# A conformer block on one core: moving batch 1's QKV into batch 0's attention, and spacing the w_pw2 tiles of the convolution

## The chip, the core and the metric

The kernel runs on one core of a Trainium2 chip. The metric is the device time of one execution in microseconds; the median of the runs is compared.

## What is computed

The reference is one conformer block on x of shape (2, 1000, 512) in bfloat16: a feed-forward half step, self-attention with four heads of 128, a convolution module with a depthwise convolution of 31 taps, a second feed-forward half step, and a final layer norm. Cut to what matters:

```python
B, T, D, K, H = (2, 1000, 512, 31, 4)
def reference(x, w_ff1a, w_ff1b, w_qkv, w_o, w_pw1, dw, w_pw2, w_ff2a, w_ff2b):
    x = x + 0.5 * (silu(layernorm(x) @ w_ff1a) @ w_ff1b)          # FF1
    qkv = layernorm(x) @ w_qkv                                    # attention
    q, k, v = ...                       # (B, H, T, 128) each
    p = softmax(einsum('bhqd,bhkd->bhqk', q, k) * 128 ** -0.5)
    att = einsum('bhqk,bhkd->bhqd', p, v)                         # back to (B, T, D)
    x = x + att @ w_o
    h = layernorm(x) @ w_pw1                                      # convolution module
    h = h[..., :D] * sigmoid(h[..., D:])
    c = sum(pad(h)[:, i:i + T, :] * dw[i] for i in range(K))
    x = x + silu(c) @ w_pw2
    x = x + 0.5 * (silu(layernorm(x) @ w_ff2a) @ w_ff2b)          # FF2
    return layernorm(x)
```

## The kernel before

The kernel is written for the five engines directly. A helper records every instruction into a list for its engine (so in the profile nearly everything has line 91 or 111, and groups are told apart by their tiles); each engine works through its list in order, and waits on semaphores of the others. T is padded to 1024, so there are 16 row tiles of 128, eight for each batch, and four column blocks of 512 tokens (nb 0 and 1 are batch 0, nb 2 and 3 batch 1). The stages run one after the other: FF1, attention of batch 0, attention of batch 1, pointwise and depthwise convolution, FF2. The residual stays in SBUF (`xres`); the normed and transposed input of each stage is `hT`.

PSUM has eight banks. QKV uses banks 0 to 3 in a ring; the scores of a unit (one head, 128 queries) take two of the banks 0 to 5; the product with V (AV) of four heads takes bank 6 or 7; out-projection and the w_pw2 tiles use "y" banks.

The attention of one batch, cut: first QKV, then 32 units of scores and AV, the AV seven units behind the scores, then the out-projection.

```python
for b in range(B):
    if b > 0:
        K.wait("act", t_av_last[b - 1])           # q, k, v buffers are reused
    for lb in range(2):                           # 16 jobs: q and k of four heads
        nb = 2 * b + lb
        for hh in range(H):
            for which in range(2):
                sl = next_ring4("pe")
                ...                               # 4 matmuls wqkv x hT, 512 columns
                ... K.emit("act", "activation", qT or kT [:, hh, ...], bank(sl), ACT.Copy ...)
    for j in range(TPB):                          # 8 jobs: v of eight row tiles
        ...                                       # 4 matmuls hT x wqkv
        t_v = K.emit("act", "activation", v_sb[:, j, :], bank(sl), ACT.Copy, sem="act")

    def do_S(u):                                  # unit u = 4 * (query tile) + head
        ss = u % 3
        K.acquire_banks("pe", [2 * ss, 2 * ss + 1])
        ...                                       # 2 matmuls of 512 columns
        t1 = K.emit("dve", "tensor_reduce", nbias..., Sv[:, 0:T], AX.X, ALU.min, sem="dve")
        te = K.emit("act", "activation", Pbuf[psl][:, 0:T], Sv[:, 0:T], ACT.Exp, ...)
        if u % 2 == 1:                            # transposes two units' probabilities
            tp = K.emit("sp", "dma_start_transpose", PTpair[pts], Ppair[pts], sem="dsp")

    def do_AV(u):
        abank = 6 + (bq % 2)                      # bq: the query tile
        K.wait("pe", t_ptdma[u])
        if hh == 0:
            K.acquire_banks("pe", [abank])
        ...                                       # 8 matmuls of 128 columns
        if hh == H - 1:                           # after four heads
            ...                                   # dve: reciprocal, four tensor_scalar into atok
            ...                                   # sp: dma_start_transpose of atok into attT

    for step in range(NU + L):                    # NU = 32 units, L = 7
        if step < NU:
            do_S(step)
        if step - L >= 0:
            do_AV(step - L)
        hook(("unit", b, step))                   # batch 0: norms of row tiles 12 to 15

    for j in range(TPB):                          # out-projection of eight row tiles
        ...                                       # 4 matmuls attT x wo
        ...                                       # dve: add into xres; then norm statistics
```

The FF2 weights are loaded into the tiles `w_a` and `w_b`, which FF1 used, as soon as FF1 is done:

```python
ff_phase([], lambda i: tile_done(i, 12), ff1_hook)
rel1 = slab_release()
K.waits("sp", rel1)
t_w["w_a"] = [K.emit("sp", "dma_start", w_a[...], wav2[...], sem="dsp") for hf in range(2)]
t_w["w_b"] = K.emit("sp", "dma_start", w_b[:], ..., sem="dsp")
attn_phase(rel1, lambda i: tile_done(i, 12), attn_hook)
rel2 = slab_release()
conv_phase(rel2, lambda i: tile_done(i, 8), conv_hook)
```

The depthwise convolution runs in four iterations of 512 tokens. Each loads shifted copies of the gated input by DMA (`load_g4`, one iteration ahead), runs eight groups of 16 tap matmuls on PE, then a silu (four sigmoids on ScalarE, four products on VectorE). The w_pw2 tiles of the iteration before, which read its silu, are put between the tap groups:

```python
for it, (b, tb) in enumerate(iters):
    banks = [0, 1, 2, 3] if it % 2 == 0 else [4, 5, 6, 7]
    ybanks = [4, 5] if it % 2 == 0 else [0, 1]
    if it + 1 < len(iters):
        load_g4(it + 1)                           # waits for the taps of it - 1
    pend = ...                                    # the four w_pw2 tiles of it - 1
    K.acquire_banks("pe", banks)
    K.waits("pe", t_g4[it])
    for m in range(NTG):                          # NTG = 8 tap groups
        ...                                       # 16 matmuls
        if pend and m % 2 == 1:
            pw2_tile(pend.pop(0), ybanks)         # 4 matmuls, then dve adds into xres, norm
    for i in range(4):
        ts = K.emit("act", "activation", sig[:, ss, :], bank(banks[i]), ACT.Sigmoid, sem="act")
        tm = K.emit("dve", "tensor_tensor", sT[:, i, ...], bank(banks[i]), sig[:, ss, :], ALU.mult, sem="dve")
```

Of the kernel before, what the change touches and what calls it, by code (L numbers as in the profile page):

```python
# [5 lines left out]
ACT = mybir.ActivationFunctionType  # L6
# [5 lines left out]
B = 2  # L12
T = 1000
D = 512
KCONV = 31
H = 4
DH = D // H
TP = 1024
DC = D // 128
F = 4 * D  # L20
# [3 lines left out]
TPB = TP // 128  # L24
# [6 lines left out]
SCALE = float(DH) ** -0.5  # L31
# [105 lines left out]
def bass_standalone__conformer_family_zipformer__speech_kernel(  # L137
# [13 lines left out]
    with ExitStack() as es:  # L151
# [42 lines left out]
        attT = big[0][:, 0:H * B * TP].rearrange("p (h t) -> p h t", h=H)  # L194
        qT = big[1][:, 0:H * TP].rearrange("p (h t) -> p h t", h=H)
        kT = big[1][:, H * TP:2 * H * TP].rearrange("p (h t) -> p h t", h=H)
        dw_sb = big[2][:, 0:D]
        NP = 8
        Pbuf = [big[2][:, s_ * TP:(s_ + 1) * TP] for s_ in range(NP)]
# [11 lines left out]
        def bank(b):  # L211
            return ps[:, b, :]
# [31 lines left out]
        t_w = {}  # L244
# [165 lines left out]
        def hT_ready(eng, nb):  # L410
            for lt in range(4):
                K.wait(eng, t_tr[nb * 4 + lt])
# [68 lines left out]
        def attn_phase(slab_waits, on_tile_done, hook):  # L481
# [12 lines left out]
            t_attT = {}  # L494
            t_av_last = {}

            for b in range(B):
                if b > 0:
                    K.wait("act", t_av_last[b - 1])
                t_qk = None  # L500
                for lb in range(2):
                    nb = 2 * b + lb
                    for hh in range(H):
                        for which in range(2):
                            sl = next_ring4("pe")
                            hT_ready("pe", nb)
                            col0 = which * D + hh * DH
                            t = None
                            for kc in range(DC):
                                t = K.emit("pe", "matmul", bank(sl), wqkv[:, kc, col0:col0 + DH],  # L510
                                           hT[:, kc, nb * 512:(nb + 1) * 512],
                                           start=(kc == 0), stop=(kc == DC - 1),
                                           sem=("pe" if kc == DC - 1 else None))
                            hT_readers[nb].append(t) if (hh == H - 1 and which == 1) else None
                            K.wait("act", t)
                            if which == 0:
                                t_qk = K.emit("act", "activation", qT[:, hh, lb * 512:(lb + 1) * 512], bank(sl),
                                              ACT.Copy, scale=-SCALE, sem="act")
                            else:
                                t_qk = K.emit("act", "activation", kT[:, hh, lb * 512:(lb + 1) * 512], bank(sl),  # L520
                                              ACT.Copy, sem="act")
                            K.set_bank_readers([sl], [t_qk])
                t_v = None
                for j in range(TPB):
                    i = b * TPB + j
                    nb = i // 4
                    sl = next_ring4("pe")
                    hT_ready("pe", nb)
                    t = None
                    for kc in range(DC):  # L530
                        t = K.emit("pe", "matmul", bank(sl), hT[:, kc, i * 128:(i + 1) * 128],
                                   wqkv[:, kc, 2 * D:3 * D],
                                   start=(kc == 0), stop=(kc == DC - 1),
                                   sem=("pe" if kc == DC - 1 else None))
                    hT_readers[nb].append(t) if j % 4 == 3 else None
                    K.wait("act", t)
                    t_v = K.emit("act", "activation", v_sb[:, j, :], bank(sl), ACT.Copy, sem="act")
                    K.set_bank_readers([sl], [t_v])

                hook(("qkv", b))  # L540
                units = [(qt, hh) for qt in range(TPB) for hh in range(H)]
# [4 lines left out]
                def do_S(u):  # L546
                    qt, hh = units[u]
                    ss = u % 3
                    K.acquire_banks("pe", [2 * ss, 2 * ss + 1])
                    K.wait("pe", t_qk)  # L550
                    Sv = sview(ss)
                    t = None
                    for kb in range(2):
                        t = K.emit("pe", "matmul", Sv[:, kb * 512:(kb + 1) * 512],
                                   qT[:, hh, qt * 128:(qt + 1) * 128],
                                   kT[:, hh, kb * 512:(kb + 1) * 512],
                                   start=True, stop=True, sem=("pe" if kb == 1 else None))
# [12 lines left out]
                    if u % 2 == 1:  # L570
                        K.wait("sp", t_exp[u - 1])
                        K.wait("sp", te)
                        pts = psl // 2
                        K.waits("sp", pt_readers[psl - 1] + pt_readers[psl])
                        tp = K.emit("sp", "dma_start_transpose", PTpair[pts], Ppair[pts], sem="dsp")
                        p_readers[psl - 1] = [tp]
                        p_readers[psl] = [tp]
                        t_ptdma[u - 1] = tp
                        t_ptdma[u] = tp

                def do_AV(u):
                    qt, hh = units[u]
                    bq = b * TPB + qt
                    abank = 6 + (bq % 2)
                    pts = u % NPT
                    K.wait("pe", t_ptdma[u])
                    K.wait("pe", t_v)
# [3 lines left out]
                    t = None  # L591
                    for kc in range(TPB):
                        t = K.emit("pe", "matmul", av[:, hh * DH:(hh + 1) * DH], PT[pts][:, kc, :],
                                   v_sb[:, kc, hh * DH:(hh + 1) * DH],
                                   start=(kc == 0), stop=(kc == TPB - 1),
                                   sem=("pe" if kc == TPB - 1 else None))
                    pt_readers[pts] = [t]
# [63 lines left out]
        def conv_phase(slab_waits, on_tile_done, hook):  # L661
# [97 lines left out]
            for it, (b, tb) in enumerate(iters):  # L759
# [25 lines left out]
                t_taps[it] = t  # L785
                K.wait("act", t)
# [34 lines left out]
        def slab_release():  # L821
            return [("pe", K.cnt["pe"])] + [t_x[i] for i in range(NTILE)]
# [17 lines left out]
        def ff1_hook(ev):  # L840
# [4 lines left out]
            elif ev == ("ffa_done", 1):  # L845
                for i in range(12, 16):
# [4 lines left out]

        ff_phase([], lambda i: tile_done(i, 12), ff1_hook)
        rel1 = slab_release()
        K.waits("sp", rel1)
        wav2 = w_ff2a.rearrange("(kc p) f -> p kc f", p=128)
        t_w["w_a"] = [K.emit("sp", "dma_start", w_a[:, :, hf * (F // 2):(hf + 1) * (F // 2)],
                             wav2[:, :, hf * (F // 2):(hf + 1) * (F // 2)], sem="dsp") for hf in range(2)]
        t_w["w_b"] = K.emit("sp", "dma_start", w_b[:], w_ff2b.rearrange("(fc p) d -> p fc d", p=128), sem="dsp")

        def attn_hook(ev):  # L860
            if ev[0] == "unit" and ev[1] == 0 and ev[2] in (2, 4, 6, 8):
# [2 lines left out]
        attn_phase(rel1, lambda i: tile_done(i, 12), attn_hook)  # L864
        assert [d[0] for d in deferred] == [12, 13, 14, 15]
        rel2 = slab_release()

        def conv_hook(ev):
            if ev[0] == "pw1" and ev[1] in (1, 2):
# [48 lines left out]
```

## Time and profile before

| | |
|---|---|
| median of 4 runs | 572.95 us (572.51 to 574.88) |
| profiled span | 570.7 us |
| PE busy | 443.1 us, 78% |
| VectorE busy | 331.2 us, 58% |
| ScalarE busy | 264.6 us, 46% |
| GpSimd busy | 81.0 us, 14% |
| mean granted PE clock | 0.953 |

The stages in the profiled execution, from its timeline: FF1 to 148, attention of batch 0 from 148 to 244, attention of batch 1 from 244 to 334, the pointwise part of the convolution from 334 to 371, the taps from 376 to 435, FF2 from 440 to the end at 570.7 us.

In the lines of a profile, PE is TensorE's matmuls and PEld its weight loads, DVE is VectorE, ACT ScalarE, POOL GpSimd, and SPq the queue of SyncE that issues DMAs. A timeline line has the start, the duration, the engine, the program's line, the operation, the output and input tiles with their shape and the number of instructions merged; in square brackets stands the idle time before it and what ended it. `big` is any of four large buffers that different stages use for different things (in attention: q, k, the probabilities and their transposes; in the convolution: the gated input, its shifted copies and the silu). A busy share is an average; where an engine is in order, its idle time before one instruction tells more than its share.

### The profile page before, as it was taken

The numbers are of one execution on the slowest core, as the hardware profiler recorded it, in microseconds if no ns is written. First come the engines' busy times: TensorE is split into PE (matmuls) and PEld (weight loads), VectorE is DVE, ScalarE is ACT, GpSimd is POOL, SyncE is SP. The second block draws the span as 40 slices with busy tenths as digits, with TensorE's granted clock in tenths as the row PEclk, the third lists the DMA queues.
The fourth block names the chain that finished last, engine by engine and source line by source line (L and its number), as shares of the span: only waits on it lengthen the run. The fifth ranks groups of instructions, "written<-read, shape, count | busy, mean of one in ns | idle before, by whom it ended". The sixth has DMA issues, their size and how long they took to land. (4 is left out here: it accounts for less than half of the span.)

```text
span 570.7 us, 7590 instructions
## 1 busy us (share of the span) xinstructions
PE 443.1 (78%) x2673; PEld 203.6 (36%) x2720; DVE 331.2 (58%) x741; ACT 264.6 (46%) x428; POOL 81.0 (14%) x231
## 2 busy tenths in 40 slices
PE   1596999999995565788665687867877649999995
PEld 1242444334442344333343432333222214444442
DVE  4276765797219886633988355206534667575743
ACT  3656553432379764167876144202322455353522
POOL 3201311101002000220000023404400210202021
PEclk9998999999999998799999699879888999999998
DMA  8801150102447999320999632969910120001011
GB/s 280 270 2 37 39 165 20 28 1 46 162 134 130 175 176 175 65 48 0 187 179 181 117 47 36 205 110 175 184 29 1 28 46 2 28 2 37 1 35 45
DMA packets 125034, 51.75 MB, mean 91 GB/s; under 512 B 107653, under 2 KB 120900, under 8 KB 124996
## 3 DMA queue, kind: packets, MB, share of 16 engines
q1 hardware_dynamic: 123460, 46.84, 38.6%
q0 software_dynamic: 1536, 4.43, 3.8%
q8 instruction: 21, 0.34, 0.2%
q14 instruction: 17, 0.14, 0.1%
HBM read 14.14 MB, written 2.05 MB: 28 GB/s over the span
## 5 line engine op out<-in xcount | busy, mean ns | idle before, releaser
L111 DVE TENSOR_TENSOR big<-ps,sig 128x512 bf16<-128x512 f32 (+1 forms) x160 | 106.8, 686 | 79.1 <-ACT sig L111 78.9
L111 ACT ACTIVATE sig<-ps 128x512 bf16<-128x512 f32 x160 | 91.2, 595 | 79.3 <-PE ps L111 70.2
L91 PE MATMUL ps<-hT,w_a 128*128 128x512 bf16 x373 | 104.6, 389 | 20.9 <-DVE big L111 19.2
L91 PE MATMUL ps<-w_b,big 128*128 128x512 bf16 x470 | 107.8, 379 | 0.5
L111 DVE TENSOR_REDUCE nbias<-ps 128x1 f32<-128x1000 f32 x64 | 73.3, 1191 | 46.6 <-PE ps L111 46.5
L111 ACT ACTIVATE hbf<-xres,nmr,rstd 128x512 bf16<-128x512 f32 x48 | 39.0, 812 | 110.9 <-DVE nmr L111 110.9
L111 ACT ACTIVATE big<-ps,nbias 128x1000 bf16<-128x1000 f32 x64 | 70.0, 1094 | 24.9 <-DVE nbias L111 24.6
L111 POOL TENSOR_TENSOR veps<-mv,consts 128x1 f32<-128x1 f32 x80 | 15.4, 192 | 440.1 <-DVE nmr L111 258.7
L91 PE MATMUL ps<-v_sb,big 128*128 128x128 bf16 x448 | 40.3, 240 | 37.9 <-DMA big<-big 37.9
L91 PEld LDWEIGHTS ps<-w_b,big 128*128 128x128 bf16 x480 | 46.9, 98 | 56.7 <-DVE xres L111 0.4
L91 PEld LDWEIGHTS ps<-hT,w_a 128*128 128x128 bf16 x384 | 36.4, 100 | 73.2 <-DVE big L111 31.8
L91 PEld LDWEIGHTS ps<-v_sb,big 128*128 128x128 bf16 x448 | 32.1, 108 | 57.5 <-DMA big<-big 51.3
L111 PE MATMUL ps<-hT,w_a 128*128 128x512 bf16 x128 | 49.5, 386 | 0.3
L111 DVE BATCH_NORM_STATS2 bnst<-xres 128x6 f32<-128x512 f32 x64 | 44.2, 691 | 1.5
L111 POOL TENSOR_TENSOR rstd<-veps,consts 128x1 f32<-128x1 f32 x80 | 44.1, 551 | 6.2
L91 PE MATMUL ps<-big,W 128*32 128x512 bf16 x508 | 34.6, 424 | 7.3 <-DMA big<-big 6.5
L111 DVE TENSOR_TENSOR xres<-ps,xres 128x512 f32<-128x512 f32 x32 | 22.0, 689 | 25.2 <-PE ps L111 25.0
L111 ACT ACTIVATE big<-xres,nmr,rstd 128x512 bf16<-128x512 f32 x16 | 13.0, 813 | 48.9 <-DVE nmr L111 48.9
L91 PE MATMUL ps<-hT,wpw 128*128 128x512 bf16 x109 | 28.0, 396 | 6.1 <-DVE big L111 3.9
L91 PE MATMUL ps<-big 128*128 128x512 bf16 x54 | 20.9, 387 | 11.5 <-ACT big L111 10.6
L111 DVE SCALAR_TENSOR_TENSOR xres<-ps,xres 128x512 f32<-128x512 f32 x16 | 11.1, 691 | 29.3 <-PE ps L111 29.3
L91 PE MATMUL ps<-hT,wqkv 128*128 128x512 bf16 x94 | 25.5, 379 | 1.0 <-ACT big L111 1.0
(66 smaller groups left out, 413.8 us busy)
## 6 DMA issues: line engine op xcount, KB each, us to landing
big<-big POOLq DMA_DIRECT2D x32, 135.0 KB, 5.2
big<-big SPq DMA_DIRECT2D x32, 135.0 KB, 6.9
w_a<-in_w_ff1a_dram SPq DMA_DIRECT2D x2, 1024.0 KB, 8.4
w_b<-in_w_ff1b_dram SPq DMA_DIRECT2D x1, 2048.0 KB
w_a<-in_w_ff2a_dram SPq DMA_DIRECT2D x2, 1024.0 KB, 8.0
w_b<-in_w_ff2b_dram SPq DMA_DIRECT2D x1, 2048.0 KB, 13.4
big<-in_x_dram SPq DMA_DIRECT2D x14, 128.0 KB, 6.1
out_dram<-big SPq DMA_DIRECT2D x14, 128.0 KB
```

Of the source, the lines that this page charges most:

```text
L91: self.q[eng].append(lambda e, m=method, a=args, k=kw: (m(e, *a, **k) if callable(m) else getattr(e, m)(*a, **k)))
L111: lambda e, m=method, a=args, k=kw, h=h, n=n: (m(e, *a, **k) if callable(m) else getattr(e, m)(*a, **k)).then_inc(h, n)
```

## The change

It does three things.

1. QKV of batch 1 is cut into 24 jobs, and these are put into the unit loop of batch 0: one after every second step from 6 to 28 (in PSUM bank 7), and two after each step from 32 on, when no scores are left to compute (in banks 0 to 3). For batch 1, V is copied out of PSUM by VectorE instead of ScalarE. Batch 0's AV then has bank 6 alone. It is meant to use PE time that the unit loop leaves idle.
2. Both batches' q, k and v now live at the same time, so batch 1's take the tiles `w_a` and `w_b`, and the FF2 weights are loaded after the attention instead of before it.
3. In the convolution, the four w_pw2 tiles follow tap groups 3, 4, 5 and 6 instead of 1, 3, 5 and 7, so that the silu they read has more time to be done.

The diff, cut:

```diff
+        w_a_flat = w_a[:].rearrange("p a b -> p (a b)")
+        qT1 = w_a_flat[:, 0:H * TP].rearrange("p (h t) -> p h t", h=H)
+        kT1 = w_a_flat[:, H * TP:2 * H * TP].rearrange("p (h t) -> p h t", h=H)
+        v1 = w_b[:, 0:TPB, :]
...
-            for b in range(B):
-                if b > 0:
-                    K.wait("act", t_av_last[b - 1])
...
+            def job_bank():
+                if job_step[0] is None:
+                    return next_ring4("pe")
+                sl = 7
+                K.acquire_banks("pe", [sl])
+                return sl
+
+            def qkv_jobs(b):
+                ...                       # qk_job: 4 matmuls, ScalarE copy, as before
+                    def v_job(j, nb=nb):
...
+                        if b == 0:
+                            tv = K.emit("act", "activation", vb_[b][:, j, :], bank(sl), ACT.Copy, sem="act")
+                        else:
+                            tv = K.emit("dve", "tensor_copy", vb_[b][:, j, :], bank(sl), sem="dve")
...
+            pending_qkv = {1: qkv_jobs(1)}    # for each lb: 8 q and k jobs, then 4 v jobs
+            for b in range(B):
+                if b == 0:
+                    for job in qkv_jobs(0):
+                        job()
+                else:
+                    while pending_qkv[1]:
+                        pending_qkv[1].pop(0)()
...
-                    abank = 6 + (bq % 2)
+                    abank = 6 + (bq % 2 if b else 0)
...
                     hook(("unit", b, step))
+                    if b == 0 and 6 <= step < 30 and step % 2 == 0:
+                        job_step[0] = step
+                        pending_qkv[1].pop(0)()
+                        job_step[0] = None
+                    if b == 0 and step >= 32:
+                        for _ in range(2):
+                            if pending_qkv[1]:
+                                pending_qkv[1].pop(0)()
...
-                    if pend and m % 2 == 1:
+                    if pend and m in (3, 4, 5, 6):
                         pw2_tile(pend.pop(0), ybanks)
...
         rel1 = slab_release()
-        K.waits("sp", rel1)
-        t_w["w_a"] = ...                  # the FF2 weight loads
-        t_w["w_b"] = ...
         attn_phase(rel1, lambda i: tile_done(i, 12), attn_hook)
         rel2 = slab_release()
+        K.waits("sp", rel2)
+        t_w["w_a"] = ...
+        t_w["w_b"] = ...
```

More of the change, by code (lines that the diff above doesn't have):

```diff
@@ L495, in attn_phase @@
             t_av_last = {}
-            for b in range(B):
-                if b > 0:
-                    K.wait("act", t_av_last[b - 1])
-                t_qk = None
+            qTb = [qT, qT1]
+            kTb = [kT, kT1]
+            vb_ = [v_sb, v1]
+            t_qk_b = {}
+            t_v_b = {}
+            job_step = [None]
+            def job_bank():
[4 more added lines that the diff above has]
+                return sl
@@ L501, in attn_phase, with qk_job @@
+            def qkv_jobs(b):
+                jobs = []
                 for lb in range(2):
                     nb = 2 * b + lb
+                    def qk_job(hh, which, nb=nb, lb=lb):
+                        sl = job_bank()
+                        hT_ready("pe", nb)
+                        col0 = which * D + hh * DH
+                        t = None
+                        for kc in range(DC):
+                            t = K.emit("pe", "matmul", bank(sl), wqkv[:, kc, col0:col0 + DH],
+                                       hT[:, kc, nb * 512:(nb + 1) * 512],
+                                       start=(kc == 0), stop=(kc == DC - 1),
+                                       sem=("pe" if kc == DC - 1 else None))
+                        hT_readers[nb].append(t)
+                        K.wait("act", t)
+                        dst = (qTb[b] if which == 0 else kTb[b])[:, hh, lb * 512:(lb + 1) * 512]
+                        if which == 0:
+                            tq = K.emit("act", "activation", dst, bank(sl), ACT.Copy, scale=-SCALE, sem="act")
+                        else:
+                            tq = K.emit("act", "activation", dst, bank(sl), ACT.Copy, sem="act")
+                        K.set_bank_readers([sl], [tq])
+                        t_qk_b[b] = tq
+                    def v_job(j, nb=nb):
+                        i = b * TPB + j
+                        sl = job_bank()
+                        hT_ready("pe", nb)
+                        t = None
+                        for kc in range(DC):
+                            t = K.emit("pe", "matmul", bank(sl), hT[:, kc, i * 128:(i + 1) * 128],
+                                       wqkv[:, kc, 2 * D:3 * D],
+                                       start=(kc == 0), stop=(kc == DC - 1),
+                                       sem=("pe" if kc == DC - 1 else None))
+                        hT_readers[nb].append(t)
+                        if b == 0:
+                            K.wait("act", t)
+                            tv = K.emit("act", "activation", vb_[b][:, j, :], bank(sl), ACT.Copy, sem="act")
+                        else:
+                            K.wait("dve", t)
+                            tv = K.emit("dve", "tensor_copy", vb_[b][:, j, :], bank(sl), sem="dve")
+                        K.set_bank_readers([sl], [tv])
+                        t_v_b[b] = tv
@@ L503, in attn_phase @@
                     for hh in range(H):
                         for which in range(2):
[L505 to L538, printed above, removed]
+                            jobs.append(lambda hh=hh, which=which, f=qk_job: f(hh, which))
@@ new lines, in qkv_jobs @@
+                    for j in range(4 * lb, 4 * lb + 4):
+                        jobs.append(lambda j=j, f=v_job: f(j))
+                return jobs
+            pending_qkv = {1: qkv_jobs(1)}
[3 more added lines that the diff above has]
+                        job()
+                else:
+                    while pending_qkv[1]:
+                        pending_qkv[1].pop(0)()
+                t_qk = t_qk_b[b]
+                t_v = t_v_b[b]
+                qT_, kT_, v_ = qTb[b], kTb[b], vb_[b]
@@ L554, in do_S @@
                         t = K.emit("pe", "matmul", Sv[:, kb * 512:(kb + 1) * 512],
-                                   qT[:, hh, qt * 128:(qt + 1) * 128],
-                                   kT[:, hh, kb * 512:(kb + 1) * 512],
+                                   qT_[:, hh, qt * 128:(qt + 1) * 128],
+                                   kT_[:, hh, kb * 512:(kb + 1) * 512],
                                    start=True, stop=True, sem=("pe" if kb == 1 else None))
@@ L593, in do_AV @@
                         t = K.emit("pe", "matmul", av[:, hh * DH:(hh + 1) * DH], PT[pts][:, kc, :],
-                                   v_sb[:, kc, hh * DH:(hh + 1) * DH],
+                                   v_[:, kc, hh * DH:(hh + 1) * DH],
                                    start=(kc == 0), stop=(kc == TPB - 1),
@@ L853, in bass_standalone__conformer_family_zipformer__speech_kernel @@
         rel1 = slab_release()
-        K.waits("sp", rel1)
[L855 to L858, printed above, removed]
         def attn_hook(ev):
@@ L866, in bass_standalone__conformer_family_zipformer__speech_kernel @@
         rel2 = slab_release()
+        K.waits("sp", rel2)
+        wav2 = w_ff2a.rearrange("(kc p) f -> p kc f", p=128)
+        t_w["w_a"] = [K.emit("sp", "dma_start", w_a[:, :, hf * (F // 2):(hf + 1) * (F // 2)],
+                             wav2[:, :, hf * (F // 2):(hf + 1) * (F // 2)], sem="dsp") for hf in range(2)]
+        t_w["w_b"] = K.emit("sp", "dma_start", w_b[:], w_ff2b.rearrange("(fc p) d -> p fc d", p=128), sem="dsp")
         def conv_hook(ev):
```

## The prediction

> **What bounds the kernel now.** I first read the page's slices for the TensorE clock and the idle stretches, then cut the span into stages with the stretches view, then read the waits and the timeline inside the stages that the change touches.
>
> The stretches view, one row per stage. Its columns are: us, PE, PE weight loads, VectorE, ScalarE and GpSimd busy (instructions), granted clock, DMA share, GB/s.
>
> ```profile
> 148.20:169.00 20.80, 20.69 (x96) 9.40 (x97) 1.80 (x9) 13.73 (x23) 0.49 (x8) 1.00 0.61 202
> 169.00:219.50 50.50, 29.14 (x252) 16.57 (x255) 43.77 (x68) 39.02 (x66) 2.97 (x8) 0.97 0.88 157
> 219.50:232.90 13.40, 6.82 (x65) 5.98 (x66) 4.29 (x14) 2.37 (x4) 0.00 (x0) 0.63 0.84 146
> 232.90:244.20 11.30, 9.25 (x32) 3.20 (x32) 10.24 (x28) 3.25 (x4) 3.71 (x10) 0.83 0.24 46
> 244.20:266.10 21.90, 20.75 (x95) 9.29 (x96) 3.13 (x9) 15.62 (x26) 2.23 (x6) 1.00 0.13 25
> 266.10:313.50 47.40, 29.08 (x268) 16.32 (x271) 42.83 (x62) 35.83 (x63) 0.00 (x0) 1.00 0.93 163
> ...
> 375.80:434.60 58.80, 45.21 (x554) 17.98 (x560) 25.53 (x52) 14.64 (x24) 14.73 (x32) 0.91 0.56 105
> ```
>
> In order these are QKV of batch 0, its 32 attention units, their drain, its out-projection, QKV of batch 1, the units of batch 1, and the convolution taps. QKV is pure PE work (20.75 of 21.90 us) with VectorE and the DMA nearly idle. The unit loop is the opposite: VectorE is 87 to 90% busy, the DMA share is 0.88 to 0.93 and PE is only 58 to 61% busy. So the loop has PE time to give away and almost none elsewhere. What PE waits for inside it and what ScalarE waits for (waits view, units of batch 0; total us, times, longest):
>
> ```profile
> PE ps L91 <- DMA big<-big: 12.9, 9, 2.2
> ACT big L111 <- DVE nbias L111: 11.1, 11, 1.8
> PE ps L91 <- ACT big L111: 6.9, 8, 1.4
> ```
>
> The reader is to see that PE waits for the DMA transposes of the probabilities and for the exponentials that free score banks: the loop is a ring PE, VectorE, ScalarE, DMA, PE in which no single engine is full, but VectorE and the DMA are close. The drain after it (PE timeline; start, duration, idle before):
>
> ```profile
> 220.60 0.55 PE L91 MATMUL ps<-v_sb,big 128*128 128x128 bf16 x7
> ...
> 224.83 0.93 PE L91 MATMUL ps<-v_sb,big 128*128 128x128 bf16 x7 [3.62 <-DMA big<-big]
> ...
> 230.85 0.93 PE L91 MATMUL ps<-v_sb,big 128*128 128x128 bf16 x7 [2.37 <-DMA big<-big]
> ```
>
> PE idles 6.0 us for the last transposes and the same seven matmuls stretch from 0.55 to 0.93 us. In the taps:
>
> ```profile
> 388.51 0.59 PE L91 MATMUL ps<-wpw,big 128*128 128x512 bf16 x2 [1.80 <-DVE big L111]
> ...
> 403.68 0.79 PE L91 MATMUL ps<-wpw,big 128*128 128x512 bf16 x2 [2.58 <-DVE big L111]
> 404.26 0.63 PE L111 MATMUL ps<-wpw,big 128*128 128x512 bf16 x1
> 404.83 3.14 PE L91 MATMUL ps<-big,W 128*32 128x512 bf16 x32
> ...
> 420.49 0.59 PE L91 MATMUL ps<-wpw,big 128*128 128x512 bf16 x2 [3.20 <-DVE big L111]
> 420.92 0.54 PE L111 MATMUL ps<-wpw,big 128*128 128x512 bf16 x1
> 421.39 3.39 PE L91 MATMUL ps<-big,W 128*32 128x512 bf16 x32
> ```
>
> Each time the first w_pw2 tile, queued after two taps, stops the in-order PE until VectorE has finished the activated sum (silu) of the iteration before, and the 32 tap matmuls after the second and third stop take 3.14 and 3.39 us where others take 1.91.
>
> **What the Trainium skill says.** "TensorE: Matmul & The Clock Gate", Part 1: the PE clock falls to half after an idle window of about 3.4 us and rises after as long a busy one. The trace agrees: clock 0.63 in the drain, and the 1.91 us group at 3.14 to 3.39 us behind gaps of 2.6 to 3.2 us. The same page, "Architectural detail": ScalarE and VectorE queues are strictly first in, first out, so a copy for batch 1 that stands in their queue delays the exponential or reduction behind it; the trace has each engine's work in program order. "VectorE: DVE Perf Modes", "Why PSUM operands drop a tier": an fp32 operand in PSUM gets the basic rate, so the new VectorE copy of V should cost what a 128x512 fp32 PSUM operation costs here, 0.69 us. "DMA: Bandwidth & Descriptors", "Issuing engines are not separate DMA queues": all transfers share 16 engines, so weights and transposes slow each other if they meet; before, they did not meet (weights inside QKV of batch 0, DMA share 0.61).
>
> **The change, part by part.**
>
> *Removed:* the stage 244.2 to 266.1, -21.9 us. Its 96 matmuls come back elsewhere: 24 jobs of 4, at 0.865 us each (20.75/24).
>
> *Loop of batch 0.* Twelve jobs enter at steps 6 to 28: 10.4 us more PE, 8 ScalarE copies at 0.597 (+4.8 us), 4 VectorE copies at 0.69 (+2.8 us). Four units need: PE 4 x (0.43 + 0.44) = 3.5 us, with two jobs 5.2 us; VectorE 4 x 1.11 (the spacing of back-to-back reductions) + 1.3 (reciprocal and four scalings) = 5.7 us, plus V copies in some; the DMA 2 transposes of 512 KB at the peak rate of about 210 GB/s (2.5 us each) plus a small one, 5.9 us. The loop takes 50.5/8 = 6.3 us. PE thus still fits, but loses the slack with which it now catches up after a late transpose. Batch 0 also gets one AV bank instead of two (bank 7 goes to the jobs), so each group's first AV must wait out the 1.3 us eviction. I charge the 2.8 us on VectorE in full, since it is the tightest queue, and choose 1.7 us for the rest: +4.5 us.
>
> *Drain of batch 0.* Twelve jobs, two after each of the first six of the seven last AVs (units 25 to 30). From 220.6: the AV of 0.44 us, then jobs 1.73 us to 222.8, wait for the transpose at 224.8, then five more AVs with five pairs (5 x 2.17 = 10.9 us) and a last AV 0.44: about 236.1 against 232.9 now. The idle 6.0 us is filled and the clock should stay up. +3.2 us.
>
> *Start of batch 1.* Scores now follow the out-projection directly. The two last tiles' additions and norm statistics run on VectorE until 247.5, under QKV today; now the first reduction waits for them, and the norm's transposes meet the first probability transposes. +2 us.
>
> *Weights.* The FF2 weights move from 149.3 to the end of attention, because their tiles now hold batch 1's q, k and v. Before (issues view):
>
> ```profile
> w_a<-in_w_ff2a_dram SPq DMA_DIRECT2D x2, 1024.0 KB, 8.0
> w_b<-in_w_ff2b_dram SPq DMA_DIRECT2D x1, 2048.0 KB, 13.4
> ```
>
> That is 4 MB done about 15 us after the first issue. In old times they would start at about 336 under the pointwise stage (334.5 to 371), end near 351, and be needed at 440. The first norm transpose of that stage comes at 348.4 and its consumer only at 362. +0.5 us.
>
> *w_pw2 tiles after taps 3, 4, 5, 6 instead of 1, 3, 5, 7.* An iteration holds 8 x 0.95 (taps) + 4 x 0.95 (tiles) = 11.4 us. Four taps last 3.8 us, and the silu chain takes 0.6 + 2.5 = 3.1 us: it fits, where two taps (1.9 us) did not. The last tile also ends one tap earlier, so the norm ahead of the sigmoids starts earlier. Walking through: taps of iteration 1 end at 396.2; iteration 2 still starts at 399.2 because its shifted copies land about 398; it ends at 410.6; iteration 3 stalls about 1 us and ends at 422.9 to 423.1; its silu is done at 426.5 where it is 434.6 now. That is -8.1 us; I keep 0.6 us back for half clock after the 3 us gap at 396: -7.5 us.
>
> Sum: -21.9 + 4.5 + 3.2 + 2.0 + 0.5 - 7.5 = -19.2 us, so 572.95 becomes about 554 us.
>
> **The rivals.** *The ring tightens.* With PE, VectorE and DMA all near 6 us per four units, waits stop overlapping: a score held behind a job delays its reduction, its exponential, its transpose, and the AV seven units later. For it: PE already waits 12.9 us on transposes in this loop. Against it: PE keeps about 1 us per four units. It would cost 8 to 12 us more, giving 562 to 566. *The jobs are hidden better than I think.* If the DMA is the true pacer (share 0.88, over 1.0 in many slices), work on the other engines only fills waits: loop +1, drain +2, giving about 548. *The weights collide.* They might hold back the transposes of the last four tiles and then the shifted copies of iteration 0 (issued at about 354 to 357, DMA share about 1.0 until 375). For it: that stretch already ends on DMA. Against it: by rate they are done before it. It would cost 4 to 6 us, about 559. *The pw2 gain is swallowed* by the shifted copies of iteration 3, which land only about 12 us after the taps of iteration 1: then the gain is 4 us, about 557.
>
> **Range and chances.** The sure part is large: 21.9 us of exclusive PE time vanishes, and a stall of 2 to 3 us per tap iteration has a plain cause. The uncertain part is the loop, +1 to +14 us. 546 to 564 should hold it 8 times in 10. The 2% mark is 561.5 us; it takes the first rival nearly in full, or two of the others at once, to miss it: faster 0.85, same 0.12, slower 0.03.
>
> **What would show it.** In the profile after: no stretch of QKV matmuls between the out-projection and the scores of batch 1; the loop of batch 0 at 53 to 57 us instead of 50.5; the drain at 16 to 17 us with a clock near 1; FF2 weights landing about 15 us into the pointwise stage with no PE wait on them; the taps and their last silu lasting about 50.7 us instead of 58.8, with no wait on VectorE's silu above about 1 us inside them. I am wrong if the loop grows by more than 9 us, if QKV work reappears as PE waits on bank 7, if batch 1's units slow as well, or if the tap stage starts its iterations on late copies.

## The result and the profile after

The changed kernel takes 551.14 us (median of 11 runs, 548.09 to 554.06) against 572.53 us for the kernel before in the same comparison; the ratio is 0.9629, 95% interval 0.9606 to 0.9652. The profiled span went from 570.7 to 549.3 us. The prediction was 554 us, 546 to 564.

The stretches view of the kernel after, one row per stage: units of batch 0, their drain, batch 1 from its first scores to its out-projection, the pointwise stage, and the taps up to the first matmul behind the last silu. Columns as before: us, PE, PE weight loads, VectorE, ScalarE and GpSimd busy, clock, DMA share, GB/s.

```profile
167.96:220.20 52.24, 38.59 (x299) 21.32 (x303) 46.43 (x72) 42.66 (x73) 2.97 (x8) 0.97 0.92 154
220.20:236.33 16.13, 14.22 (x112) 8.29 (x113) 6.60 (x16) 7.44 (x14) 0.00 (x0) 1.00 0.61 117
...
247.50:307.98 60.48, 39.02 (x317) 22.80 (x322) 48.02 (x79) 38.94 (x67) 2.22 (x6) 0.85 0.93 164
...
318.53:359.80 41.27, 30.06 (x127) 12.48 (x128) 14.88 (x29) 12.97 (x21) 12.79 (x40) 0.94 0.92 212
359.80:411.65 51.85, 42.83 (x554) 17.53 (x561) 25.62 (x52) 14.53 (x24) 14.72 (x32) 0.95 0.69 119
```

The out-projection of batch 0 fills 236.33 to 247.50, and batch 1's scores follow it at once: there is no QKV stage between them any more. The same cuts in both timelines, from first matmul to first matmul:

| stage | before, us | after, us | difference | predicted |
|---|---|---|---|---|
| units of batch 0, first to last score | 50.4 | 52.2 | +1.9 | +4.5 |
| drain, to the out-projection | 13.6 | 16.1 | +2.5 | +3.2 |
| out-projection of batch 0 | 11.2 | 11.2 | 0 | 0 |
| QKV of batch 1 | 21.9 | 0 | -21.9 | -21.9 |
| batch 1, first score to out-projection | 57.9 | 60.5 | +2.6 | +2.0 |
| out-projection and pointwise stage | 51.8 | 51.8 | 0.0 | +0.5 (weights) |
| taps to the matmul behind the last silu | 58.8 | 51.9 | -6.9 | -7.5 |
| all the rest | 305.0 | 305.6 | +0.6 | 0 |

What PE waits for in the units of batch 0 (waits view, after; total us, times, longest):

```profile
PE ps L91 <- DVE atok L111: 4.5, 4, 1.4
PE ps L91 <- ACT big L111: 4.3, 5, 1.4
PE ps L91 <- DMA big<-big: 2.8, 3, 1.3
```

Against the 12.9 us on transposes of before, only 2.8 us are left; 4.5 us are now for the eviction of the single AV bank. PE busy went from 29.1 to 38.6 us in nearly the same time: the jobs stand where the wait for the transposes stood. In the drain (PE timeline) the seven matmuls of an AV keep 0.55 us and have no idle time in brackets, the gaps between them being the pairs of jobs:

```profile
225.02 0.55 PE L91 MATMUL ps<-v_sb,big 128*128 128x128 bf16 x7
227.19 0.55 PE L91 MATMUL ps<-v_sb,big 128*128 128x128 bf16 x7
```

At the start of batch 1, the last norm of the out-projection and the first reductions on VectorE (timeline, after):

```profile
250.18 0.69 DVE L111 BATCH_NORM_STATS2 bnst<-xres 128x6 f32<-128x512 f32 x1
...
251.06 12.80 DVE L111 TENSOR_REDUCE nbias<-ps 128x1 f32<-128x1000 f32 x11
```

and in the timeline of before, when VectorE had stood idle behind QKV:

```profile
266.76 8.94 DVE L111 TENSOR_REDUCE nbias<-ps 128x1 f32<-128x1000 f32 x8 [19.29 <-PE ps L111]
```

The first scores start at 247.50, their reduction at 251.06, 3.6 us later; before, the two starts were 0.6 us apart (266.13 and 266.76). The eleventh reduction ends 16.4 us after the first score starts, where it was 13.5 us, and VectorE is busy for 15.7 of the 16.4 us. In the taps (PE timeline, after):

```profile
383.39 3.64 PE L91 MATMUL ps<-big,W 128*32 128x512 bf16 x64 [2.66 <-DMA big<-big]
...
396.11 3.64 PE L91 MATMUL ps<-big,W 128*32 128x512 bf16 x64 [1.28 <-DMA big<-big]
400.71 0.59 PE L91 MATMUL ps<-wpw,big 128*128 128x512 bf16 x2 [0.97 <-DVE big L111]
```

Four tap groups now run in one piece at 3.64 us; the stops of 1.80, 2.58 and 3.20 us for the silu are down to one of 0.97 us. What ends the gaps now is the landing of the shifted copies. The FF2 weights (issues view, after) land as fast as before:

```profile
w_b<-in_w_ff2b_dram SPq DMA_DIRECT2D x1, 2048.0 KB, 13.5
```

"All the rest" holds one difference that is not the change's. FF2 took 130.8 us before and 132.5 us after. Both have the same stop of 2.66 us ahead of the same matmuls; behind it the granted clock fell to half for 3.4 us in this execution and stayed full in the other (stretches view, first after, then before; each row is 3.41 us long):

```profile
443.63:447.04 3.41, 0.75 (x4) 0.31 (x4) 1.54 (x4) 3.18 (x6) 0.48 (x1) 1.00 0.42 63
447.04:450.46 3.42, 3.42 (x9) 1.22 (x8) 2.11 (x4) 1.25 (x3) 0.00 (x0) 0.50 0.09 16
```

```profile
465.39:468.80 3.41, 1.44 (x7) 0.48 (x5) 1.12 (x6) 2.20 (x4) 0.74 (x2) 1.00 0.17 32
468.80:472.21 3.41, 2.72 (x13) 1.29 (x14) 3.21 (x6) 2.57 (x5) 0.00 (x0) 1.00 0.28 54
```

In the profiles of all the kernels below, FF2 takes 130.8 us or 132.2 to 132.5 us, and 132.5 also where nothing but one PSUM bank of the attention was changed. The loops differ between profiles too: where the code up to the loop's end is the same, by 0.2 us (the kernel before and the first experiment) and by 0.6 us (the changed kernel and the third). So differences between kernels of 1 to 2 us are looked for in their stages first, and less than 1 us in one stage shows little.

### The profile page after: what moved, and what is told of

Same layout as the page of the kernel before. It is cut to its first block, busy times and chain, and to the rows that moved or that the text cites. A ratio compares the mean times of both kernels' runs of the same rounds, so it can differ in the third digit from the quotient of the medians.

```text
span 549.3 us, 7593 instructions
## 1 busy us (share of the span) xinstructions
PE 441.2 (80%) x2674; PEld 202.0 (37%) x2720; DVE 337.0 (61%) x749; ACT 259.5 (47%) x420; POOL 81.0 (15%) x231
## 3 DMA queue, kind: packets, MB, share of 16 engines
HBM read 14.14 MB, written 2.05 MB: 29 GB/s over the span
## 5 line engine op out<-in xcount | busy, mean ns | idle before, releaser
L91 PE MATMUL ps<-w_b,big 128*128 128x512 bf16 (+1 forms) x694 | 128.3, 335 | 16.3 <-DMA big<-big 15.7
L91 PEld LDWEIGHTS ps<-w_b,big 128*128 128x128 bf16 x704 | 63.3, 102 | 83.8 <-DMA big<-big 23.2
L91 PE MATMUL ps<-big,W 128*32 128x512 bf16 x508 | 33.0, 405 | 10.8 <-DMA big<-big 10.8
L91 PE MATMUL ps<-hT,wqkv 128*128 128x512 bf16 x93 | 25.8, 386 | 1.3 <-ACT w_a L111 1.2
L91 PE MATMUL ps<-v_sb,big 128*128 128x128 bf16 x224 | 18.0, 222 | 9.2 <-DVE atok L111 6.3
L91 PEld LDWEIGHTS ps<-big,W 128*32 128x32 bf16 x508 | 13.8, 101 | 29.1 <-issue 18.6
L91 DVE TENSOR_SCALAR atok<-ps,rrec 128x128 bf16<-128x128 f32 x48 | 13.9, 345 | 13.9 <-PE ps L111 12.6
## 6 DMA issues: line engine op xcount, KB each, us to landing
w_b<-in_w_ff2b_dram SPq DMA_DIRECT2D x1, 2048.0 KB, 13.5
```

The lines of the kernel that those rows point to most:

```text
L91: self.q[eng].append(lambda e, m=method, a=args, k=kw: (m(e, *a, **k) if callable(m) else getattr(e, m)(*a, **k)))
```

## The experiments

The theory: the jobs take PE time that would have been a wait for transposes, so the loop pays little for them and the drain pays only what exceeds its idle 6 us; the w_pw2 spacing is a separate gain; the weights are hidden. The rivals: the ring of the unit loop tightens; VectorE's V copies or the single AV bank cost time; the weights collide; the pw2 gain depends on the rest. Each time stands with its ratio to the kernel before, measured beside it at 572.6 to 572.8 us.

**The w_pw2 tiles alone.** The kernel before, with

```diff
-                    if pend and m % 2 == 1:
+                    if pend and m in (3, 4, 5, 6):
```

> The kernel before with only the w_pw2 tiles moved to follow tap groups 3, 4, 5, 6. If the gain is the silu wait inside the taps, as the prediction walked through: 7 us less than before, about 565.5, and the tap stage (first tap to the matmul after the last silu) 52 us instead of 58.8. Rival, the gain needs the earlier weights or an idle DMA that the rest of the change brings, or is swallowed by late shifted copies: 2 to 4 us less, about 569.

Measured: 566.5 us, ratio 0.9885 (0.985 to 0.992), 6.3 us less. From the first tap to FF2 the profile has 56.3 us instead of 64.0. The theory's size, without any of the rest of the change.

**The weights alone.** The kernel before, with

```diff
-        K.waits("sp", rel1)
-        t_w["w_a"] = ...   # and t_w["w_b"]
         attn_phase(rel1, lambda i: tile_done(i, 12), attn_hook)
         rel2 = slab_release()
+        K.waits("sp", rel2)
+        t_w["w_a"] = ...   # and t_w["w_b"]
```

> The kernel before with only the FF2 weight loads moved behind the attention. If 4 MB land in about 15 us under the pointwise stage: no difference, 572.5 within 1 us. Rival, they hold back the last four norm transposes or the shifted copies: 3 to 6 us more.

Measured: 572.54 us, ratio 0.9987 (0.9971 to 1.0003). Nothing lost. The waits of PE in the pointwise stage show why nothing shows; first of the kernel before, then with the weights late:

```profile
PE ps L91 <- DMA big<-big: 5.1, 1, 5.1
PE ps L91 <- DMA hT<-hbf: 2.0, 1, 2.0
```

```profile
PE ps L91 <- DMA big<-big: 7.0, 1, 7.0
PE ps L91 <- DMA hT<-hbf: 0.4, 1, 0.4
```

PE waits less for the norm's transposes and correspondingly longer for the shifted copies, which end the stage in either case.

**QKV and weights without the w_pw2 spacing.** The changed kernel, with

```diff
-                    if pend and m in (3, 4, 5, 6):
+                    if pend and m % 2 == 1:
```

> The changed kernel with the w_pw2 tiles back behind tap groups 1, 3, 5, 7. If the parts add up: 7 us more than the changed kernel, about 558, so the moved QKV alone is worth about 14 us. Rival, the parts help each other: 560 or more, or 555 or less.

Measured: 559.25 us, ratio 0.9762 (0.9735 to 0.9789), 8 us above the changed kernel and 13.6 us (2.38%) below the kernel before. The product of this ratio and that of the w_pw2 tiles alone, 0.9762 x 0.9885, is 0.9650, inside the interval of the changed kernel (0.9606 to 0.9652): the parts add up within what is measured.

**One AV bank alone.** The kernel before, with

```diff
-                    abank = 6 + (bq % 2)
+                    abank = 6 + (bq % 2 if b else 0)
```

> The kernel before with batch 0's AV in bank 6 alone, nothing else. If the wait for the bank only takes the place of the wait for the transpose behind it: within 1 us of before, with PE waits on atok of 4 to 5 us in the loop and about as much less on the transposes. Rival, the single bank is a cost of its own: 2 us or more over before in the loop of batch 0.

Measured: 572.77 us, ratio 1.0005 (0.9991 to 1.0018). PE's waits in its unit loop:

```profile
PE ps L91 <- DVE atok L111: 9.6, 5, 3.6
...
PE ps L91 <- DMA big<-big: 4.9, 3, 2.1
```

The new wait of 9.6 us takes the place of 8 us on transposes (12.9 to 4.9). The loop is 1.8 us longer and the drain 2.9 us shorter (10.7 us), so the bank moves time from one to the other and costs nothing in sum. The rival's 2 us in the loop would have looked nearly right from the loop alone.

**All 24 jobs in the loop.** The changed kernel, with

```diff
-                    if b == 0 and 6 <= step < 30 and step % 2 == 0:
+                    if b == 0 and 6 <= step < 30:
```

> The changed kernel with all 24 jobs in the unit loop, one after every step from 6 to 29, none in the drain. If the loop has idle PE time left (19 us before, 10.4 used): the drain goes back to about 13.4 us from 15.9, the loop grows by 1 to 2 us, so about 550, 1 us less than the changed kernel. Rival, the ring tightens once PE has no slack to catch up after a late transpose: loop 5 us or more longer, 554 to 558.

Measured: 559.87 us, ratio 0.9782 (0.9754 to 0.981), 9 us more than the changed kernel; the theory's expectation missed. The drain is 12.7 us, but the loop 65.4 us. PE is busy for 49.7 us of it, so it isn't full. The PE timeline of three jobs in a row; between them, left out, lie the scores and the AV of each step:

```profile
196.26 0.59 PE L91 MATMUL ps<-hT,wqkv 128*128 128x512 bf16 x2 [0.60 <-ACT w_a L111]
...
198.22 0.82 PE L91 MATMUL ps<-hT,wqkv 128*128 128x512 bf16 x3 [0.26 <-ACT w_a L111]
...
200.50 0.82 PE L91 MATMUL ps<-wqkv,hT 128*128 128x512 bf16 x3 [0.37 <-ACT w_a L111]
```

and ScalarE in the same stretch:

```profile
197.57 0.59 ACT L111 ACTIVATE w_a<-ps 128x512 bf16<-128x512 f32 x1
198.78 1.09 ACT L111 ACTIVATE big<-ps,nbias 128x1000 bf16<-128x1000 f32 x1 [0.62 <-DVE nbias L111]
...
199.86 0.59 ACT L111 ACTIVATE w_a<-ps 128x512 bf16<-128x512 f32 x1
```

Each job waits for the copy that empties bank 7. The copy of the job at 198.22 could run when the job ends, at about 199.3, but it stands behind the exponential of its step (198.78), which waits for VectorE's reduction of scores that themselves stood behind the job before. So the job at 200.50 hangs on the one at 196.26, two steps before it, through scores, reduction, exponential and copy: 4.2 us for two steps. In this loop PE waits 8.1 us for the copies and never for the transposes. In the changed kernel there are two steps from job to job, so the chain has twice the room, and PE waits 1.2 us for a copy. The chain is read from the trace: no run gave the jobs a second bank.

**No job in the loop.** The changed kernel, with

```diff
-                    if b == 0 and 6 <= step < 30 and step % 2 == 0:
+                    if False:
...
-                        for _ in range(2):
+                        for _ in range(4):
```

> The changed kernel with no job in the loop and all 24 in the drain, four after each of six AVs. If jobs in the loop are nearly free and the drain hides only its 6 us of idle PE: loop 1 to 2 us shorter, drain 10.4 us longer, about 560. Rival, the loop is what pays for the jobs: 553 or less.

Measured: 562.35 us, ratio 0.9819 (0.9794 to 0.9844), 11 us more than the changed kernel. The loop is 51.3 us, so twelve jobs cost the loop 0.9 us by this profile; the run with one AV bank alone, whose loop has no jobs either, took 52.2 us, against which they cost nothing. The drain is 28.1 us, 12.0 us more for twelve more jobs, one microsecond each (stretches view, drain):

```profile
219.40:247.50 28.10, 26.16 (x160) 13.86 (x162) 9.22 (x20) 12.64 (x22) 0.00 (x0) 0.94 0.41 66
```

PE is busy for 26.2 of the 28.1 us: beyond its idle time, the drain pays for jobs in full.

**V copied by ScalarE.** The changed kernel, with

```diff
-                        if b == 0:
+                        if True:
                             K.wait("act", t)
```

> The changed kernel with batch 1's V copied out of PSUM by ScalarE as in the kernel before. If VectorE is the tightest queue of the loop, as the prediction charged (2.8 us for four copies): 1 to 2.5 us less than the changed kernel. Rival, VectorE's copies fall into waits and ScalarE is as tight: no difference, within 0.7 us.

Measured: 549.58 us, ratio 0.9593 (0.9566 to 0.962), 1.6 us below the changed kernel; the two intervals overlap. The profile doesn't find the gain where the expectation put it: the loop is 51.1 us instead of 52.2, but the drain 18.0 instead of 16.1. From the first score of batch 0 to the last out-projection it takes 140.5 us, the changed kernel 140.0. The profiled span is 1.4 us shorter, and its FF2 is the short kind of 130.8 us. So it isn't shown that the four VectorE copies cost anything in sum.

**Two scores ahead of the out-projection.** The changed kernel, with

```diff
-                    if step < NU:
+                    if step < NU and not (b == 1 and step < 2):
                         do_S(step)
...
+                if b == 0:                # with batch 1's q and k
+                    do_S(0)
+                    do_S(1)
                 for j in range(TPB):      # out-projection
```

> The changed kernel with the first two score units of batch 1 put before batch 0's out-projection. If batch 1's units pay 2.6 us because their first reduction waits behind the out-projection's norm statistics: 1.5 to 3 us less than the changed kernel. Rival, VectorE is full from the drain to the tenth reduction whatever the order, so nothing is won: within 0.7 us.

Measured: 551.99 us, ratio 0.9645 (0.9617 to 0.9672): no gain, the rival. VectorE's timeline shows the exchange:

```profile
239.27 2.30 DVE L111 TENSOR_REDUCE nbias<-ps 128x1 f32<-128x1000 f32 x2
241.48 0.68 DVE L111 TENSOR_TENSOR xres<-ps,xres 128x512 f32<-128x512 f32 x1
...
254.46 8.94 DVE L111 TENSOR_REDUCE nbias<-ps 128x1 f32<-128x1000 f32 x8 [0.19 <-PE ps L111]
```

The two reductions push the additions and norms 2.2 us later, and the next eight reductions with them. VectorE is busy for 25.8 of the 26.8 us from 238 on. From the first score of batch 0 to the last out-projection the profile has 139.9 us, the changed kernel's 140.0. The 2.6 us of batch 1 are VectorE's own work that used to lie under QKV, and this order doesn't hide it.

**16 jobs in the loop, 8 in the drain.** The changed kernel, with

```diff
-                    if b == 0 and 6 <= step < 30 and step % 2 == 0:
+                    if b == 0 and 6 <= step < 30 and step % 3 != 1:
```

> The changed kernel with 16 jobs in the loop (two of every three steps from 6 to 29) and 8 in the drain. If the loop with 24 jobs was slow because each job must wait for bank 7, which is freed only after the exponential ahead of its copy: two jobs in a row meet that wait too, loop 3 to 5 us longer, drain 2 us shorter, about 553. Rival, it was slow because PE was full: three steps with two jobs need 4.35 us of PE against 4.7 us that they take, so the loop stays within 1 us and the time is about 549.5.

Measured: 552.61 us, ratio 0.9646 (0.9619 to 0.9674). The loop is 57.8 us, 5.6 more than in the changed kernel, the drain 12.9, 3.2 less. PE is busy for 44.7 us of the 57.8, and waits 3.6 us for ScalarE's copies, up to 2.1 us at a time. So a full PE is out. The wait for bank 7 grew as expected, but by 2.4 us (from 1.2), less than half of the loop's 5.6. The loop also has 10.2 us of half clock in this profile, against 3.4 in the changed kernel's (mean clock 0.91 and 0.97), and how the rest divides isn't shown.

**All 24 jobs in the loop, ahead of the scores.** The run with 24 jobs in the loop, with the block that emits the job moved up:

```diff
+                    if b == 0 and 6 <= step < 30:
+                        ...               # the job
                     if step < NU:
                         do_S(step)
                     if step - L >= 0:
                         do_AV(step - L)
-                    if b == 0 and 6 <= step < 30:
-                        ...
```

> All 24 jobs in the loop, but each put ahead of its step's scores instead of behind its AV, so that its copy stands in ScalarE's queue ahead of that step's exponential. If the wait for bank 7 was the larger part of the 13 us that 24 jobs cost in the loop: PE waits on the copies gone, steps of 1.75 to 1.85 us instead of 2.2, loop 57 to 59 us instead of 65.4, about 553. Rival, a full PE alone: loop still 63 us or more, 558 to 560.

Measured: 561.36 us, ratio 0.9796 (0.9761 to 0.9831), the loop 66.7 us with 9.7 us of waits for the copies. The edit was badly chosen. A job ahead of the scores of step s is the same as a job behind the AV of step s - 1, in PE's queue and in ScalarE's: the order of the two queues is that of the run it was to be compared with, one step earlier. It repeats that run and tells nothing between the two expectations.

**Job first, V by ScalarE, 12 jobs in the loop.** The changed kernel, with

```diff
-                        if b == 0:
+                        if True:
                             K.wait("act", t)
...
+                    if b == 0 and 6 <= step < 30 and step % 2 == 0:
+                        ...               # the job, ahead of do_S(step)
```

> The changed kernel (12 jobs in the loop, 12 in the drain) with each job of the loop ahead of its step's scores and V copied by ScalarE. If copies on VectorE cost 1.6 us as measured and the bank wait about 1 us: 548.5 to 549.5. Rival, putting the copy ahead of the exponential delays the ring: 551 or more.

Measured: 552.97 us, ratio 0.9656 (0.9628 to 0.9683), above the run with V by ScalarE alone, whose interval ends at 0.962. As just said, the edit moves the jobs by one step, from even to odd ones. The loop is 55.5 us instead of 51.1, and PE waits 10.1 us for the AV bank instead of 4.8. These two runs differ in the position alone, so the position makes the difference. Why is a reading: every second job of the even steps stands right behind the AV that completes a bank, in the time in which VectorE empties it; in the odd steps none does. This loop also has 6.8 us of half clock, the other none.

**The same with 16 jobs.** That kernel, with

```diff
-                    if b == 0 and 6 <= step < 30 and step % 2 == 0:
+                    if b == 0 and 6 <= step < 30 and step % 3 != 1:
```

> As the run before it, with 16 jobs in the loop and 8 in the drain. If PE still has room in the loop at 16 jobs and the drain gets 2 us back: 547 to 548.5. Rival, the ring has no room for more than 12: 551 or more.

Measured: 548.43 us, ratio 0.9578 (0.9552 to 0.9604), the fastest of all; its interval just clears that of the changed kernel. But its loop and drain take 54.7 and 14.8 us, together 1.1 us more than the changed kernel's 68.4, and its profile has the shorter FF2 (130.8 us) and is 2.0 us shorter from the first tap to FF2. So the gain is measured and its cause isn't found. This loop also warns against reading the wait for bank 7 as lost time: PE waits 7.0 us for the copies here and 3.6 us in the earlier run with 16 jobs in the loop, whose loop is 3.1 us longer; here the clock is full throughout.

## Why the prediction was right, step by step

The forecast was -19.2 us, and -21.4 us came. By the table, the loop, the drain and the weights were charged 3.8 us too much, the start of batch 1 and the taps 1.2 us too little, and the rest grew by 0.6 us.

**QKV of batch 1, -21.9 us: right.** The stage is gone, and nothing of it came back as a stage. The run without the w_pw2 spacing nets 13.6 us for it where the prediction's terms net 11.7 (21.9 - 4.5 - 3.2 - 2.0 - 0.5).

**The loop, +4.5: right in kind, too large.** It measured +1.9. The prediction said that "PE still fits, but loses the slack", and charged the 2.8 us of V copies on VectorE (0.69 us each, as they then took) in full plus 1.7 us for the rest. The failing term is the full charge: 12 jobs with their copies cost the loop at most 0.9 us over a loop with one AV bank and no jobs (52.2 against 51.3 and 52.2), and taking the V copies off VectorE gave the loop 1.1 us and took it back in the drain. A queue that is 87% busy in a ring still has waits that work can fall into. The charge for the AV bank was about right for the loop (+1.8 in the profile with nothing else changed, +1.0 in the one with all jobs in the drain) but is no cost: the drain returned it.

**The drain, +3.2: right**, +2.5, by the walk described: idle time filled, clock at 1.00, two jobs between AVs. The only remaining wait was not foreseen: 1.8 us on the AV bank at its start.

**Start of batch 1, +2.0: right**, +2.6, by the stated cause. The other half of the sentence, that the norm's transposes meet the first probability transposes, is not needed: VectorE is busy for 15.7 of the first 16.4 us.

**Weights, +0.5: right** in saying hidden; measured alone, no difference.

**w_pw2 tiles, -7.5: right**, -6.9 in the stage and -6.3 us alone. Each item of the walk is found: a gap ahead of iteration 2 (2.66 us on late copies, walked as 3.0), about 1 us of silu wait in iteration 3 (0.97), and no half-clock tap group behind the stops of iterations 1 to 3. (The start of iteration 0 is at half clock before and after.) The gap ahead of iteration 3 (1.28 us on copies) was missed. What the 0.6 us kept back stood for didn't come: the taps behind the 2.66 us gap ran at full clock.

**The rivals.** "The ring tightens" didn't happen with 12 jobs, and does with 16 and 24; but not as described, by PE, VectorE and DMA all near 6 us, but with 24 by one bank that is freed in ScalarE's order, as far as a trace shows it, and with 16 only in part by that. (The DMA's 5.9 us would be 5.6 by the rate that the prediction names: two transposes of 2.5 us and one of a quarter of the size.) The prediction had named "PE waits on bank 7" only among the signs of being wrong; the changed kernel has 1.2 us of it, the one with 24 jobs 8.1 us. "Hidden better than I think" is closer to what the loop did. The collision of the weights is out. The late shifted copies came, but took little of the w_pw2 gain.

**The signs.** Two of the signs of being wrong came without harm: iterations 2 and 3 of the taps start on late copies, which the prediction's own walk had for iteration 2, and batch 1 slowed, by about what was charged. The loop stayed below the 53 to 57 us that were to show it. The 50.7 us for the taps were the walk without the 0.6 us kept back; 51.9 came.

**The clock and the queues.** "TensorE: Matmul & The Clock Gate", Part 1, of the Trainium skill gives an idle window of about 3.4 us; the traces don't agree with that length. Before the change, stops of 2.58 and 3.20 us in the taps were already followed by half clock, where the prediction saw agreement, and in FF2 one stop of 2.65 to 2.67 us was followed by half clock in eight profiles and by full clock in six, with the same instructions. The last section says what told them apart. The strict order of ScalarE's queue (the same page, "Architectural detail") turned out to carry more than the prediction made of it: it is what ties a job to the exponential ahead of its copy.

## What to carry to other kernels

Work moved into an engine's waits was nearly free here until the jobs stood so close that their own bank closed a new ring: follow a filler job's bank through the queue of the engine that empties it, and space the jobs by that chain rather than by the idle time of the filled engine. When a wait in the profile gets a new name, compare the whole phase with its drain before calling it a cost. And a consumer that stands too early in an in-order queue is cured by moving it behind work that needs no wait: here two more tap groups, for over 6 us.

## What was not expected of the hardware

The FF2 stage, the same in all these kernels, took 130.8 us in six profiles and 132.2 to 132.5 us in eight: up to 1.7 us of a kernel's time that no edit made. In each of the 14 profiles the changes of the granted clock lie on a grid of 3.41 us: that is the shortest stretch of half clock, and the others are multiples of it, but for the last, which the end of the kernel cuts. The grid falls differently on each execution. The stop in FF2 is as long in all, but where 2.1 to 2.7 us of it fall into one interval of the grid, the next interval has half clock (the eight), and where the grid cuts it so that no interval gets more than 2.0 us, the clock stays full (the six). Over the whole of the 14 profiles, no interval at full clock with under 1.7 us of idle PE was followed by half clock, and all 119 with more than 2.05 us were; in between both occur. So it was not the length of a stop that told what the clock did, but how much idle time fell into one interval.
